# A re-ordered list of work in a fused softcap attention and maxout feed-forward kernel

## The chip, the cores and the metric

The kernel runs on one core of one Trainium2 chip. The metric is the device time of one execution in microseconds (us), the median over several runs. The kernel before takes 328.32 us (three runs, 328.07 to 328.5).

## What is computed

```python
scores = q @ k.T / sqrt(64)                # 8 batches, 12 heads, 448 x 448
scores = 30 * tanh(scores / 30)
attn   = softmax(scores)                   # over the keys
x      = (attn @ v), heads side by side    # 3584 tokens x 768
g      = maximum(x @ w1, x @ w2)           # 3584 x 1024
out    = g @ w_out                         # 3584 x 768
```

## The kernel before

**One list sets all order.** No scheduler moves anything: the string `ORDER` is a list of some 2,300 short entries, and a loop at its end calls one small function for each entry. Each function issues its instructions to fixed engines, so an engine's queue holds its instructions in the order of the list, and each engine works through its queue from the front. A dependency between two engines becomes a semaphore wait at the later instruction. The kernel is written with the identity max(a, b) = relu(a - b) + b, so that w1 - w2 feeds a relu and w2 times w_out is multiplied out beforehand.

**Units.** `t` counts 24 groups of four heads, `i` = 2t or 2t+1 counts pairs of two heads, and `g` counts 120 feed-forward groups, 14 for an even batch and 16 for an odd one.

**Entries of the attention.**
- `ld0`, `cd`: the first pairs of q and k are loaded and cast (`cd k` on VectorE, others on ScalarE). `lq`, `lk`, `lv`, `lw1`, `lw2`, `lwo` are loads by GpSimd's queue (L317, L336, L357, L364, L389).
- `X i bank` (and `Xh i c` for one half) turns q and k of a pair on TensorE (L446) for the first ten pairs, `XC` copies the result out (VectorE). From t = 5 on, `cr t` (L473) does the turning with one DMA transpose that SyncE's queue issues at L475.
- `S i j`: two score matmuls (L514) into one of only two score tiles in PSUM. `T i j` is their tanh on ScalarE (L519), `L t` and `TL t` the same for the last 64 keys (L528, L532). `E i j0 j1` and `EL t` are the exponentials on ScalarE (L536, L539). A score tile is free again when its tanh has read it.
- `A`, `B` add exponentials (VectorE), `Y` sums them on TensorE (L566, L573), `Y1` to `Y3` turn and invert the sums (VectorE), `VL`, `V` are the matmuls with v (L600, L606), and `N t u` writes the normalized result `xT` (VectorE, L618, L621).

**Entries of the weights.** `W c` turns a block of w2 on TensorE (L416), `WC` copies it out, `OP` and `P c half n` multiply it with w_out (L431), `PC` copies that out, `sub` forms w1 - w2 (VectorE). `D bank n` issues matmuls on a constant tile (L471) that only keep TensorE at work in the first 16 us.

**Entries of the feed-forward part.** `O g bank` opens group g in one of four PSUM banks. `M x y n` makes n steps, and a step is two matmuls at once (L645): one of group x on array rows 0 to 63 and one of group y on rows 64 to 127. So a group runs one half of its work on the lower rows, then the other on the upper rows, or the reverse. Both halves add into the same bank. `M x x n` uses all 128 rows (L640, the last two groups). `ev g` copies a finished group out on VectorE (L666, L702), `eva g` on ScalarE (L700). `st b t` stores rows of the output, two DMAs from SyncE's queue (L676 to L681).

**The hand-over.** When a group changes rows, its next matmul may have to wait until its last matmul on the other rows has ended. For that the entry `Hs g` puts a `nop` on SyncE's queue that waits for that last matmul, and the group's next matmul waits for the nop; `H g` puts the nop on VectorE's queue instead (L654). Where the list has no such entry ahead of a change of rows, no such wait is made (the test of `self.turn` in `step`). The list of before holds 107 `Hs` and 21 `H` for 145 changes of rows.

Of the kernel before, what the change touches and what calls it, by code (L numbers as in the profile page):

```python
# [14 lines left out]
P 1 0 4; P 3 0 2; OP 2 0 3; P 2 0 7; P 1 0 1; P 2 0 1; P 1 0 1; P 3 0 2; P 1 0 2; PC 2 0; PC 1 0; E 1 2 3;  # L15
E 1 0 2; TL 1; T 2 0; EL 0; S 3 0; S 2 2; P 3 0 1; W 0 2; P 3 0 1; X 4 3; T 2 2; T 3 0; VL 0; Y 0 1; V 0 0 0 3;
V 0 1 0 3; S 3 1; lwo 1 0; lwo 1 1; lq 5 0; lk 5 0; lv 1 0; lv 1 1; lk 8 0; lq 8 0; lq 7 0; lw2 4; lv 6 2; lq 6 0;
lk 7 0; lk 6 0; lw2 5; lw1 2; lw1 4; lw1 0; lv 2 0; lv 2 1; WC 0; PC 3 0; XC 4; Y1 0; Y2 0; Y3 0; N 0 0; N 0 1;
E 2 0 3; T 3 1; EL 1; E 3 0 2; OP 0 0 1; P 0 0 2; OP 2 1 2; P 2 1 2; P 0 0 1; OP 1 1 3; P 1 1 2; P 0 0 1; P 1 1 2;
P 0 0 1; P 1 1 4; S 4 0; S 3 2; X 5 0; P 2 1 4; P 0 0 3; P 2 1 1; XC 5; PC 1 1; PC 0 0; T 3 2; T 4 0; E 3 2 3;  # L20
OP 3 1 3; P 3 1 1; P 2 1 1; S 4 1; S 4 2; Y 1 1; T 4 1; T 4 2; L 2; P 3 1 4; VL 1; TL 2; V 1 1 0 3; V 1 0 0 3;
S 5 0; X 6 0; E 4 0 3; T 5 0; EL 2; Y1 1; Y2 1; PC 2 1; Y3 1; N 1 1; N 1 0; XC 6; X 7 2; W 4 1; S 5 2; S 5 1;
X 8 0; P 3 1 3; WC 4; XC 8; PC 3 1; T 5 1; T 5 2; OP 4 0 1; P 4 0 2; OP 0 1 0; P 0 1 3; S 6 0; S 6 1; W 5 3;
P 0 1 1; P 4 0 6; P 0 1 4; E 5 0 2; T 6 1; T 6 0; E 5 2 3; XC 7; sub 2 0; WC 5; sub 4 0; PC 4 0; sub 0 0; PC 0 1;
OP 5 1 3; P 5 1 4; S 6 2; L 3; Y 2 1; T 6 2; TL 3; E 6 0 3; VL 2; V 2 1 0 1; V 2 0 0 3; V 2 1 1 3; S 7 0; P 5 1 4;
OP 5 0 0; P 5 0 8; Y1 2; Y2 2; Y3 2; N 2 0; N 2 1; A 3 0 1; A 3 0 2; PC 5 1; PC 5 0; T 7 0; EL 3; lk 9 0; lq 11 0;
lv 3 1; lq 9 0; lw1 1; lw1 3; lq 10 0; lk 12 1; lv 3 0; lw1 5; lk 10 0; lk 11 0; lk 11 1; lk 10 1; S 7 2; O 0 1;
M 0 -1 2; S 7 1; M 0 -1 4; O 1 2; M 1 -1 1; T 7 2; T 7 1; Hs 0; M 1 -1 1; S 8 1; M 1 -1 1; M 1 0 3; S 8 0; X 9 3;
OP 4 1 0; P 4 1 4; sub 1 0; sub 3 0; XC 9; T 8 1; E 7 0 2; T 8 0; E 7 2 3; P 4 1 4; L 4; O 2 3; M 2 0 3; S 8 2;
M 2 1 3; A 3 1 1; B 3 1; PC 4 1; ev 0; B 3 0; Hs 2; TL 4; T 8 2; O 3 0; M 3 1 3; M 3 2 1; S 9 0; M 3 2 2; T 9 0;  # L30
E 8 0 3; ev 1; A 3 1 2; sub 5 0; cr 5; Hs 3; O 4 1; M 4 2 1; VL 3; V 3 0 0 3; Y 3 2; V 3 1 0 3; M 4 2 2; S 9 1;
M 4 3 3; lk 13 0; lk 13 1; lv 4 1; lv 4 0; lv 5 3; lv 5 0; lq 13 0; lq 15 0; lq 12 0; lk 12 0; lk 15 1; Y1 3;
Y2 3; Y3 3; ev 2; Hs 4; O 5 2; M 5 3 3; M 5 4 3; T 9 1; EL 4; ev 3; N 3 0; N 3 1; Hs 5; O 6 3; M 6 4 3; M 6 5 2;
S 10 0; M 6 5 1; O 7 0; M 7 5 3; Hs 6; ev 4; A 4 0 1; ev 5; M 7 6 2; S 9 2; M 7 6 1; Hs 7; cr 6; E 9 0 2; T 10 0;
T 9 2; O 8 1; M 8 6 3; S 10 2; M 8 7 3; S 10 1; O 9 2; M 9 7 1; T 10 2; T 10 1; E 9 2 3; M 9 7 2; VL 4; V 4 0 0 2;
L 5; TL 5; A 4 1 1; H 8; A 4 0 2; B 4 1; ev 7; B 4 0; A 4 1 2; ev 6; M 9 8 3; V 4 1 0 3; Y 4 0; V 4 0 2 3;
# [12 lines left out]
M 16 14 1; st 0 1; M 16 14 1; Hs 15; T 14 1; cr 8; B 6 0; M 16 15 1; S 14 2; M 16 15 1; ev 14; M 16 15 1; T 14 2;
O 17 2; M 17 15 2; H 16; M 17 15 1; B 6 1; M 17 16 2; E 13 2 3; M 17 16 1; ev 15; O 18 3; M 18 16 1; L 7; VL 6;  # L50
A 6 1 2; st 0 2; TL 7; V 6 0 0 2; V 6 1 0 2; Y 6 0; E 14 0 3; V 6 0 2 3; V 6 1 2 3; Y1 6; S 15 0; M 18 16 1;
lv 8 0; M 18 16 1; Y2 6; M 18 17 1; Y3 6; M 18 17 1; lv 8 1; M 18 17 1; O 19 0; M 19 17 2; ev 16; Hs 18; lv 8 2;
M 19 17 1; M 19 18 1; T 15 0; N 6 0; M 19 18 2; lv 8 3; O 20 1; M 20 18 2; EL 7; Hs 19; ev 17; M 20 18 1; lk 20 0;
S 15 1; M 20 19 1; N 6 1; M 20 19 1; T 15 1; M 20 19 1; lk 20 1; O 21 2; M 21 19 3; Hs 20; M 21 20 1; lq 20 0;
ev 18; M 21 20 1; S 15 2; S 16 0; ev 19; M 21 20 1; T 15 2; O 22 3; M 22 20 1; lk 21 0; M 22 20 1; A 7 0 1; Hs 21;
M 22 20 1; M 22 21 1; E 15 0 2; M 22 21 1; lk 21 1; ev 20; S 16 1; M 22 21 1; O 23 0; M 23 21 1; A 7 0 2;
M 23 21 1; Hs 22; lq 21 0; M 23 21 1; M 23 22 2; ev 21; M 23 22 1; T 16 0; M 23 22 2; A 7 1 1; M 23 22 2; cr 9;
M 23 22 1; T 16 1; M 23 22 1; B 7 0; S 16 2; M 23 22 2; B 7 1; O 24 1; M 24 22 1; T 16 2; M 24 22 2; H 23;
M 24 23 1; H 22 2; E 15 2 3; M 24 23 2; M 22 23 1; L 8; VL 7; A 7 1 2; TL 8; V 7 0 0 2; V 7 1 0 2; Y 7 2;
E 16 0 3; V 7 0 2 3; lk 22 0; V 7 1 2 3; Y1 7; S 17 0; M 22 23 1; lv 9 0; M 22 23 1; Y2 7; M 22 23 2; Y3 7;  # L60
# [145 lines left out]
def kernel(  # L206
# [21 lines left out]
    P = 128  # L228
# [550 lines left out]
```

## Time and profile before

| | |
|---|---|
| median of three runs | 328.32 us |
| span of the profiled execution, first to last instruction | 326.9 us |
| time outside the span (the difference of the two) | 1.4 us |
| ScalarE: last exponential ends | 286.9 us |
| TensorE: last matmul ends | 322.8 us |
| VectorE: last copy of results ends | 323.4 us |
| HBM traffic over the span | 180 GB/s |

The page of the profile gives each engine's busy time; the timeline lists instructions with start and length, and in brackets how long the engine was idle before and what ended that idleness. Rows marked SPq are issues by SyncE's queue: the queue is held for the length shown. A matmul's length in the rows contains the time to pass through the array, so matmuls overlap in the rows, and the distance from start to start is what each costs.

### The profile page before, as it was taken

How to read it: one execution, taken by the hardware profiler on the slowest of the kernel's cores; microseconds unless marked ns; L12 is line 12 of the kernel's file. 1: busy time of each engine (PE TensorE's matmuls, PEld its weight loads, DVE VectorE, ACT ScalarE, POOL GpSimd, SP SyncE). 2: the span in 40 equal slices, each digit the busy share in tenths (PEclk: the TensorE clock that was granted, in tenths of full speed). 3: DMA queues.
4: the chain of work that ended last, by engine and by line, in shares of the span. 5: the costliest groups of instructions: out<-in, count | busy, mean ns of one | idle time of the engine just before them, and what ended most of it. 6: DMA issues, size and time to landing. Idle time of an engine off the chain costs nothing.

```text
span 326.9 us, 9772 instructions
## 1 busy us (share of the span) xinstructions
PE 320.2 (98%) x4138; PEld 184.5 (56%) x4138; DVE 240.1 (73%) x422; ACT 281.1 (86%) x278; POOL 162.2 (50%) x237
## 2 busy tenths in 40 slices
PE   7999999999999999999999999999999999999994
PEld 3454545545656664565565565556466556557662
DVE  3346899987997778987897788968878779773201
ACT  5999999999999999999999999999999999921120
POOL 7357584568772772764774474478448311000000
PEclk9999999999999999999999999999999999999999
DMA  8999999899999999999999999999999963013033
GB/s 179 174 202 185 269 256 112 92 140 116 221 188 98 134 182 191 102 99 175 163 176 108 208 114 181 128 140 182 183 116 101 201 156 45 2 50 98 0 98 96
DMA packets 134508, 46.28 MB, mean 142 GB/s; under 512 B 112321, under 2 KB 129473, under 8 KB 134465
## 3 DMA queue, kind: packets, MB, share of 16 engines
q0 software_dynamic: 94592, 25.02, 78.3%
q1 hardware_dynamic: 39424, 19.99, 31.1%
q8 instruction: 32, 0.52, 0.6%
q10 hardware_dynamic: 448, 0.66, 0.5%
q14 instruction: 12, 0.09, 0.1%
HBM read 47.78 MB, written 11.01 MB: 180 GB/s over the span
## 4 chain that ended last, share of the span: by engine, by line
PE 93%; DMA 3%; POOL 1%; DVE 1%; issue 0%
PE mm L645 61%; PE s L514 9%; PE s L606 9%; PE mm L431 5%; DMA w2b<-in_moe_w_dram 3%; PE s L528 2%; PE s L600 2%; PE mm L573 2%; PE mm L640 1%; POOL kqs L321 1%; PE mm L458 1%; PE mm L566 1%; PE mm L416 0%; DVE xT L621 0%; POOL w2b L366 0%; DVE xT L618 0%
## 5 line engine op out<-in xcount | busy, mean ns | idle before, releaser
L519 ACT ACTIVATE e<-s 128x896 bf16<-128x896 f32 x144 | 125.5, 927 | 5.7 <-PE s L514 5.2
L536 ACT ACTIVATE e<-e 128x1792 bf16<-128x1792 bf16 (+2 forms) x72 | 122.7, 1709 | 0.0
L645 PE MATMUL mm<-wo_sb,gT 64*128 64x384 bf16 x864 | 115.2, 323 | 0.0
L645 PE MATMUL mm<-wm_sb,xT 64*128 64x384 bf16 x648 | 102.2, 323 | 0.0
L645 PE MATMUL mm<-xT,wd_sb 64*128 64x448 bf16 x768 | 97.5, 349 | 0.0
L328 POOL DMA_DIRECT2D kqs<-in_k_dram x76 | 54.7, 722 | 56.1 <-DMA qkT<-kqs 50.9
L645 PEld LDWEIGHTS <-gT 64*128 64x128 bf16 x864 | 58.6, 94 | 25.5 <-issue 1.1
L645 PEld LDWEIGHTS <-wd_sb 64*128 64x128 bf16 x768 | 48.8, 94 | 26.7 <-issue 2.1
L645 PEld LDWEIGHTS <-xT 64*128 64x128 bf16 x648 | 50.3, 94 | 18.5 <-issue 0.2
L514 PE MATMUL s<-qkT 64*128 64x448 bf16 x288 | 52.7, 352 | 0.2 <-DVE xT L618 0.2
L352 POOL DMA_DIRECT2D vp<-in_v_dram x48 | 30.5, 639 | 32.6 <-PE s L514 23.5
L666 DVE TENSOR_SCALAR gT<-mm 128x448 bf16<-128x448 f32 x64 | 38.9, 617 | 8.7 <-PE mm L645 7.6
L328 POOL DMA_DIRECT2D kqs<-in_q_dram x38 | 35.1, 924 | 5.7 <-issue 2.5
L606 PE MATMUL s<-e,vp 128*32 128x448 bf16 x576 | 36.1, 354 | 0.0
L548 DVE TENSOR_TENSOR esum<-e 128x896 bf16<-128x896 bf16 x42 | 25.9, 617 | 9.1 <-ACT e L536 9.1
L621 DVE TENSOR_TENSOR xT<-s,inv 64x448 bf16<-64x448 f32 x48 | 29.9, 622 | 1.7 <-PE s L606 0.8
L548 DVE TENSOR_TENSOR esum<-esum,e 128x896 bf16<-128x896 bf16 x42 | 26.2, 623 | 5.9 <-ACT e L536 4.8
L514 PEld LDWEIGHTS <-qkT 64*128 64x128 bf16 x288 | 18.5, 94 | 20.1 <-issue 12.0
L700 ACT COPY osb<-mm 128x384 f32<-128x384 f32 x10 | 4.8, 479 | 26.9 <-PE mm L645 26.7
L702 DVE COPY osb<-mm 128x384 f32<-128x384 f32 x44 | 23.3, 554 | 6.2 <-PE mm L645 5.7
L553 DVE TENSOR_TENSOR esum<-esum,el 64x896 bf16<-64x896 bf16 x42 | 26.0, 619 | 1.2
L578 DVE STREAM_TRANSPOSE st<-mm 128x448 f32<-128x448 f32 x24 | 15.6, 649 | 13.0 <-PE mm L573 11.3
(57 smaller groups left out, 269.7 us busy)
## 6 DMA issues: line engine op xcount, KB each, us to landing
out_dram<-osb SPq DMA_DIRECT2D x54, 192.0 KB, 4.5
vp<-in_v_dram POOLq DMA_DIRECT2D x38, 160.0 KB, 4.3
kqs<-in_q_dram POOLq DMA_DIRECT2D x46, 112.0 KB, 5.8
kqs<-in_k_dram POOLq DMA_DIRECT2D x76, 56.0 KB, 4.4
osb<-in_moe_w_dram POOLq DMA_DIRECT2D x4, 512.0 KB, 7.4
w2b<-in_moe_w_dram POOLq DMA_DIRECT2D x6, 256.0 KB, 7.1
wo_sb<-in_moe_w_out_dram POOLq DMA_DIRECT2D x4, 384.0 KB, 9.9
vp<-in_v_dram POOLq DMA_DIRECT2D x10, 128.0 KB, 7.7
```

The costliest lines, as they stand in the source:

```text
L328: nc.gpsimd.dma_start(out=to, in_=x)
L352: nc.gpsimd.dma_start(out=to, in_=x)
L514: scored[i, j] = nc.tensor.matmul(s[:, h, :S], k_of(t, o, h, j), q_of(t, o, h)).ins
L519: nc.scalar.activation(expo[i][:, 2 * j : 2 * j + 2, :], slots[i, j][:, :, :S], AF.Tanh, scale=scale / cap)
L536: nc.scalar.activation(e, e, AF.Exp, scale=float(cap))
L548: nc.vector.tensor_add(d, e[:, 0:2, :] if j == 1 else d, e[:, 2 * j : 2 * j + 2, :])
L553: nc.vector.tensor_add(d, d, left_e[t][r, :, :])
L606: nc.tensor.matmul(vals[t][place(m, u), u, :S], w[:, m, :], expo[2 * t + o][:, 2 * j + h, :], start=False, stop=(j == NJ - 1))
L621: nc.vector.tensor_mul(x[64 - r : 128 - r], vals[t][r : r + 64, u, :S], sums[t, 3][64 - r : 128 - r])
L645: ins = nc.tensor.matmul(self.ps, w[r], x[r], start=first, stop=self.at == [self.n, self.n]).ins
L666: nc.vector.tensor_relu(gT[b // 2][:, f, cs], ps)
L702: nc.vector.tensor_copy(o[:, hs], ps)
```

## The change

The string `ORDER` is written anew, and one condition in `transposes` differs. The functions are otherwise the same, and the numbers of matmuls, tanh, exponentials, loads and stores are unchanged.

**Start.** One fragment of the list per line:

```diff
-ld0 q; ld0 q 1; cd q; ld0 k; ld0 k 1; ms; dm; ms0; cd k; id; lq 2 0; lk 3 0; lq 3 0; lk 2 0; lw2 3; lw2 2; D 3 24;
-Xh 0 0 0; Xh 0 1; cd k 1 1; cd q 1 1; XCh 0 1; XCh 0 0; D 3 4; X 1 1; S 0 0; S 0 1; XC 1; T 0 0; T 0 1; D 0 5;
-D 1 8; D 3 1; D 1 4; S 0 2; D 1 4; L 0; D 1 16; T 0 2; TL 0; E 0 0 3; D 1 12; S 1 2; S 1 0; X 3 3; X 2 0; W 3 2;
-W 2 1; T 1 0; T 1 2; lw2 1; lwo 0 0; lwo 0 1; lw2 0; lq 4 0; lk 4 0; lv 0 0; lv 0 1; XC 3; XC 2; WC 3; D 0 4;
-S 1 1; D 0 8; D 2 2; S 2 1; W 1 2; WC 2; WC 1; T 1 1; T 2 1; S 2 0; D 0 4; L 1; OP 3 0 0; P 3 0 2; OP 1 0 1;
...
+ld0 q; ld0 q 1; ld0 k; ld0 k 1; ms; dm; ms0; D 3 24; id; lq 2 0; lk 3 0; lq 3 0; lk 2 0; cd k; cd q; Xh 0 0 0;
+XCh 0 0; lw2 3; Xh 0 1 1; cd k 1 1; D 3 4; lw2 2; XCh 0 1; D 2 5; cd q 1 1; S 0 0; lw2 1; D 0 4; T 0 0; S 0 1;
+lwo 0 0; X 1 2; T 0 1; lwo 0 1; S 0 2; XC 1; X 3 3; T 0 2; lw2 0; L 0; XC 3; D 2 8; TL 0; lq 4 0; D 3 16; lk 4 0;
+E 0 0 3; D 1 4; lv 0 0; D 0 4; D 3 2; D 0 8; lv 0 1; X 2 1; lwo 1 0; S 1 0; XC 2; S 1 2; T 1 0; lwo 1 1; D 0 4;
+D 3 12; lq 5 0; T 1 2; S 1 1; lk 5 0; W 3 3; T 1 1; lv 1 0; S 2 1; WC 3; W 2 2; T 2 1; lv 1 1; S 2 0; WC 2; T 2 0;
+L 1; W 1 3; TL 1; S 2 2; WC 1; E 1 2 3; S 3 0; D 3 1; OP 2 0 1; P 2 0 1; OP 3 0 2; P 3 0 1;
...
```

The first pair's two halves now go to two banks (`Xh 0 0 0`, `Xh 0 1 1`), for which `transposes` opens a bank whenever one is named:

```diff
-        if c != 1:
+        if bank is not None:
             turned["qk", i] = mm_tile(bank).bitcast(bf16)
```

**First quarter.** Up to about t = 9 and group 30 the entries stand in a new order, on TensorE, ScalarE and VectorE alike; the order of the loads among themselves is the same. The copies of groups 25, 26 and 29 move from VectorE to ScalarE (`ev` becomes `eva`).

**Rest of the list.** From `M 28 29` on, TensorE's order is the same entry for entry, but for the bank of `Y 10` (1 becomes 3), and so is ScalarE's but for the copies named below. What differs there is where the hand-overs, the transposing DMAs and the stores stand, and on which queue a hand-over is. The new list has 98 `Hs` and 47 `H`, one for each of the 145 changes of rows. Three places of one kind:

```diff
 Hs 37; cr 12; M 38 36 1; ...; O 39 0; M 39 37 1; ev 36; M 39 37 2;
-H 38; B 10 1; E 21 2 3; M 39 38 3;
+Hs 38; B 10 1; M 39 38 1; E 21 2 3; M 39 38 2;
...
 Hs 67; cr 18; M 68 66 1; ...; O 69 1; M 69 67 1; ev 66; M 69 67 2;
-H 68; B 16 1; E 33 2 3; M 69 68 3;
+Hs 68; B 16 1; M 69 68 1; E 33 2 3; M 69 68 2;
...
-Hs 81; M 82 80 1; ...; Hs 82; ...; cr 21;
+Hs 81; cr 21; M 82 80 1; ...; Hs 82;
```

**End of the list.** The copies of groups 100, 102, 103 and 112 to 117 move from ScalarE to VectorE, and most hand-overs there from SyncE to VectorE:

```diff
-Y3 23; eva 100; M 103 101 1; M 103 102 2; eva 101; M 103 102 1; N 23 0; M 103 102 3; N 23 1;
+Y3 23; M 103 101 1; M 103 102 2; eva 101; M 103 102 1; ev 100; M 103 102 3; N 23 0; st 6 1; M 103 102 3; N 23 1;
...
-M 105 103 2; eva 102; M 105 103 1; M 105 104 2; eva 103; M 105 104 1; O 106 1; M 106 104 2; Hs 105;
+M 105 103 2; ev 102; M 105 103 1; M 105 104 2; ev 103; M 105 104 1; O 106 1; M 106 104 2; st 6 2; H 105;
...
-M 115 113 2; eva 112; M 115 113 1; M 115 114 2; eva 113; M 115 114 5; st 7 3; M 115 114 4; O 116 3;
+M 115 113 2; ev 112; M 115 113 1; M 115 114 2; ev 113; M 115 114 3; st 7 3; M 115 114 6; O 116 3;
```

More of the change, by code (lines that the diff above doesn't have):

```diff
@@ L15 @@
[L15 to L24, printed above, removed]
@@ L202 @@
+M -1 117 2; Hs 116; M -1 117 1; M 116 117 8; M -1 117 2; ev 116; M -1 117 1; O 118 1; M 118 118 1; ev 117;
+M 118 118 4; st 7 5; M 118 118 9; O 119 2; M 119 119 2; ev 118; M 119 119 12; ev 119; st 7 6;
 """
```

374 lines of the change are left out of this document (197 added, 177 removed).

## Prediction

> **What bounds the kernel now.** I read the page first, for who is busy and what chain ended last.
>
> ```profile
> span 326.9 us, 9772 instructions
> PE 320.2 (98%) x4138; PEld 184.5 (56%) x4138; DVE 240.1 (73%) x422; ACT 281.1 (86%) x278; POOL 162.2 (50%) x237
> ...
> PE 93%; DMA 3%; POOL 1%; DVE 1%; issue 0%
> ```
>
> TensorE (PE) is busy 98% of the span, and 93% of the chain that ended last is its own instructions. Next the busy time by stage (columns: stretch, its length, busy us of PE, PEld, DVE, ACT, POOL, clock, DMA share, GB/s).
>
> ```profile
> 0.00:16.00 16.00, 13.63 (x185) 6.61 (x185) 4.95 (x15) 12.05 (x14) 9.42 (x20) 1.00 0.98 175
> 16.00:48.00 32.00, 31.80 (x453) 16.64 (x453) 23.29 (x40) 31.47 (x31) 20.97 (x33) 1.00 1.26 225
> 48.00:128.00 80.00, 80.00 (x1043) 45.57 (x1045) 68.25 (x119) 78.40 (x76) 48.34 (x67) 1.00 1.35 144
> 128.00:288.00 160.00, 160.00 (x2090) 93.46 (x2086) 133.39 (x234) 154.40 (x150) 83.44 (x118) 1.00 1.17 138
> 288.00:327.00 39.00, 34.78 (x377) 22.22 (x373) 10.18 (x18) 4.79 (x10) 0.00 (x0) 0.99 0.27 70
> ```
>
> ScalarE (ACT) is nearly as full up to 288 us, but then PE works on alone for 35 us. So a lead of ScalarE is no gain by itself: the end moves only where PE starts a matmul earlier or later. The numbers of matmuls are the same in both lists, so the change is worth exactly what it does to PE's waits. The view of waits shows how few those are.
>
> ```profile
> PE mm L471 <- DVE warm L734: 1.8, 1, 1.8
> PE mm L416 <- DMA w2b<-in_moe_w_dram: 0.5, 1, 0.5
> PE s L514 <- DVE xT L618: 0.2, 1, 0.2
> ```
>
> The 1.8 us at the start stays. The other two, 0.7 us, are all that this view offers a better order; shorter waits hide in the overlap of matmuls. A new wait has no such ceiling.
>
> **First quarter.** Where its waits were and how the first scores stood (PE and ACT rows of the timeline):
>
> ```profile
> 5.26 0.39 PE L471 MATMUL mm<-warm 128*128 128x512 bf16 x1
> 5.61 0.87 PE L458 MATMUL mm<-ident,kqs 64*64 64x64 bf16 x28
> 6.42 0.55 PE L514 MATMUL s<-qkT 64*128 64x448 bf16 x4
> 6.82 2.53 ACT L519 ACTIVATE e<-s 128x896 bf16<-128x896 f32 x3 [0.80 <-PE s L514]
> 10.03 2.46 ACT L536 ACTIVATE e<-e 128x2688 bf16<-128x2688 bf16 x1
> 12.36 3.37 ACT L519 ACTIVATE e<-s 128x896 bf16<-128x896 f32 x4
> 17.98 0.98 ACT L532 ACTIVATE el<-s 128x896 bf16<-128x896 f32 x1
> 15.20 0.62 PE L416 MATMUL mm<-ident,w2b 128*128 128x128 bf16 x8 [0.52 <-DMA w2b<-in_moe_w_dram]
> 16.77 3.75 PE L431 MATMUL mm<-wo_sb,w2T 128*128 128x384 bf16 x22
> 20.45 0.55 PE L514 MATMUL s<-qkT 64*128 64x448 bf16 x4
> ```
>
> The new list puts the first scores behind two warm matmuls instead of the second pair's transposes. After the first transposes (done by 5.26) come a matmul on 512 columns and one of 512 and 128: about 0.5 us, with a change of array shape, so `S 0 0` can start at about 5.84 instead of 6.42, and the first tanh, 0.40 behind it as in the rows, at 6.24 instead of 6.82. ScalarE leads by 0.58 us.
>
> What PE makes of it: tanh follow each other at (15.55 - 12.36) / 4 = 0.80 us, an exponential on 2688 columns takes 12.36 - 10.03 = 2.33. From 6.24 on, three tanh, `TL 0`, the exponential and five tanh put `TL 1` at 15.9, and it has read its score tile at 16.84. The new list lets `S 2 2` and `S 3 0` come ahead of the first `P`, and `S 3 0` needs just that tile. So PE stands from about 16.25 to 16.88, and its first `P` comes at about 17.3 instead of 16.77: 0.5 us later, with the 0.48 us of scores at 20.45 already done. The wait of 0.52 at 15.20 has gone (`W 1 3` now comes some 0.3 us after that load), one on a score tile has come. Net zero up to here.
>
> Further on the same sum by hand (PE's entries by their rows, score tiles by the tanh that frees them) keeps both lists within 0.3 us of each other until 48 us. I take -0.3 for the whole quarter: the wait of 0.2 on `xT` goes, and a little more. The bounds: -0.7, all that the view of waits offers, to +0.9, one more wait for a score tile of the length of a `TL`.
>
> Three copies go to ScalarE at about 105 to 115 us, 0.48 us each (row below): 1.44 us. ScalarE is idle for 80.00 - 78.40 = 1.6 us between 48 and 128 us and has the lead of 0.58, so they cost nothing; without that cover PE would wait up to 1.4 us at a score tile.
>
> **Hand-overs behind the transposing DMA.** Here the change adds waits, on SyncE's queue (SPq: sequencer rows; L475 is the DMA, L654 the hand-over).
>
> ```profile
> L475 SPq DMA_TRANSPOSE qkT<-kqs x19: 1296/1655/2655, 55.3 to 262.6; - x19
> DMA to landing us min/median/max: 4.2/6.7/10.0
> ...
> 55.25 1.58 SPq L475 DMA_TRANSPOSE qkT<-kqs  x1
> L654 SPq EVENT_SEMAPHORE  x1: 17/17/17, 56.9 to 56.9; - x1
> ```
>
> The issue alone holds the queue for 1.30 to 2.66 us. The last row is the stretch from 54.9 to 57.0: no hand-over comes through until the DMA's issue ends at 56.83, then one does at 56.9. Nothing on PE waited for that one. At `cr 12` and `cr 18` before, VectorE carried the hand-over while SyncE was held:
>
> ```profile
> 134.69 1.69 SPq L475 DMA_TRANSPOSE qkT<-kqs  x1
> L654 DVEq EVENT_SEMAPHORE  x1: 21/21/21, 135.6 to 135.6; - x1
> 136.03 0.75 PE L645 MATMUL mm<-wm_sb,xT 64*128 64x384 bf16 x5
> ...
> 205.01 2.27 SPq L475 DMA_TRANSPOSE qkT<-kqs  x1
> L654 DVEq EVENT_SEMAPHORE  x1: 21/21/21, 205.9 to 205.9; - x1
> 206.37 0.75 PE L645 MATMUL mm<-wm_sb,xT 64*128 64x384 bf16 x5
> ...
> L654 SPq EVENT_SEMAPHORE  x2: 17/17/17, 237.4 to 238.6; - x2
> 238.87 1.52 SPq L475 DMA_TRANSPOSE qkT<-kqs  x1
> 239.05 0.57 PE L645 MATMUL mm<-wm_sb,xT 64*128 64x384 bf16 x4
> 160.28 1.27 SPq L681 DMA_DIRECT2D out_dram<-osb  x2
> ```
>
> The PE rows are the first matmuls that need the hand-over (groups 38, 68, 82). With `Hs 38` and `Hs 68` the nop stands behind the DMA: free at 134.69 + 1.69 = 136.38 and 205.01 + 2.27 = 207.28, plus about 0.1 to pass the nop and reach PE, so PE stands 0.45 and 1.0 us. `cr 21` now follows the hand-over at 237.4; with the same 0.27 us from hand-over to issue as at 238.6 it begins at 237.7, and the matmul at 239.05 has 1.35 us for issue and passage, as in the other two. PE's queue stops there: the matmul of the other group behind it, the scores and the sums all wait. The mean of the issues in the rows over the 1.25 us that fit is about 0.5 (19 issues: 0.05 at 1.30, 1.4 at 2.66). Three make 1.5; PE then comes later to two sums and score tiles for which it waits a little now, which I put at -0.3. Taken: +1.2. Bounds: +0.1 if all three issues are near 1.3, +3.5 if all are near 2.6. By the steps that lie between in the list, the other hand-overs behind a `cr` have over 2 us, and those behind a store about the 1.27 us that its two DMAs take; nearly all of the 17 added ones come many steps after the group's last matmul on the other rows, so their nop has long gone through. Those moved to VectorE cost it 21 ns each where it is idle 15% (68.25 of 80): zero.
>
> The Trainium skill, page "DMA: Bandwidth & Descriptors", section "Issuing engines are not separate DMA queues", speaks against this: the sequencer's time to initiate a DMA is usually small relative to the DMA. Here the row has 1.66 us of 6.7. By the page, with that time at nil, the +1.2 would be 0 and the sum 328.2; I go by the row.
>
> **End.** `ev 100` moves ahead of the last normalizations on VectorE:
>
> ```profile
> L702 DVE COPY osb<-mm 128x384 f32<-128x384 f32 x44 | 23.3, 554 | 6.2 <-PE mm L645 5.7
> L700 ACT COPY osb<-mm 128x384 f32<-128x384 f32 x10 | 4.8, 479 | 26.9 <-PE mm L645 26.7
> ...
> 291.80 1.26 DVE L621 TENSOR_TENSOR xT<-s,inv 64x448 bf16<-64x448 f32 x2
> 293.41 0.35 PE L645 MATMUL mm<-xT,wd_sb 64*128 64x448 bf16 x1
> 320.59 0.56 DVE L705 COPY osb<-mm 128x384 f32<-128x384 f32 x1 [15.46 <-PE mm L640]
> ```
>
> The normalization then ends at 293.06 + 0.55 = 293.61, and the group's sixth step at 293.41 needs it: +0.2. The other eight copies run 0.075 us longer on a VectorE that is idle for 15.46 us before the last two copies: zero, since the banks they free are taken over 1 us later.
>
> **Sum.** -0.3 + 1.2 + 0.2 = +1.1 on a span of 326.9: 328.0. Outside the span lie 328.32 - 326.9 = 1.4 us, taken as unchanged, so I set the sum against the median: 329.4.
>
> **Rivals.**
> - *The quarter pays and the hand-overs just fit.* The three issues take 1.3 us, as the quickest of the 19, and cost 0.2 together; ScalarE's lead of 0.58 takes with it the small waits on tanh that hide in overlapping matmuls, 1.0 us more beside the 0.7. For it: the lead is sure. Against: PE waited for tanh nowhere for long. 328.3 - 1.7 + 0.2 + 0.2 = 327.0.
> - *Nothing reaches the end.* The change doesn't do what it says: new waits for score tiles eat the quarter's gain, and PE, stopped at a hand-over, would have stopped at the next sum anyway. 328.4.
> - *ScalarE falls behind.* The three copies meet a ScalarE without its lead; from about 105 us each score waits until its 1.6 us of idleness have made it up. This decides if the lead at 90 us is under 0. 328.3 + 1.4 + 1.2 + 0.2 = 331.1.
>
> **How the numbers follow.** Forecast 329.4 with 0.44 (its own range 328.99 to 330.5), the quarter pays 0.22, nothing 0.22, ScalarE behind 0.12. The bound of what this measurement can tell is 0.2%, 0.66 us: 327.66 and 328.98. Faster is the first rival, 0.22; within the bound is the second and a sliver of the forecast, 0.24; slower the rest, 0.54. Signs are mixed, so the range has to reach both: from 327.1, near the first rival, to 331.2, the third.
>
> **What would show it.** In the new profile: the first tanh at about 6.2; no wait on w2b at 15.2 but PE standing before the scores near 16.5; and the three places, where the matmul of groups 38, 68 and 82 starts right behind the end of a DMA_TRANSPOSE issue. If PE runs through there while the issue is still held, the middle term is wrong; if the hand-overs stop PE and the time is still lower, the first quarter was undervalued.

## The result and the profile after

The new list takes 333.36 us (median of four runs, 333.1 to 336.2), the old one 328.28 beside it: a ratio of 1.0167, with a 95% interval of 1.0145 to 1.0188. It is slower by about 5 us, where 1.1 were forecast. (The medians alone give 1.0155; the ratio takes in the execution of 336.2 as well.) One execution of a later kernel, `e4_three_vec`, counts as slow (336.61 us) and is left out of its ratio, though not of its median. The profiled execution of after is the quickest of the four (333.1 us). First its page:

```profile
span 331.3 us, 9789 instructions
PE 321.8 (97%) x4138; PEld 188.4 (57%) x4138; DVE 243.7 (74%) x428; ACT 278.4 (84%) x272; POOL 161.7 (49%) x237
...
PE 83%; DVE 9%; ACT 3%; DMA 3%; issue 1%; SPq 0%; DVEq 0%
```

The same 4138 matmuls are spread over 4.4 us more. TensorE's own share of the chain that ended last falls from 93% to 83%, and VectorE (DVE) and ScalarE (ACT) now stand in it: TensorE has begun to wait for others. The busy time by stage says where (columns as before):

```profile
16.00:48.00 32.00, 30.86 (x453) 16.50 (x447) 22.23 (x38) 30.41 (x29) 20.91 (x33) 1.00 1.25 224
48.00:128.00 80.00, 78.69 (x992) 44.87 (x990) 65.53 (x113) 78.08 (x79) 48.08 (x67) 1.00 1.39 137
128.00:288.00 160.00, 159.13 (x2083) 91.10 (x2084) 132.49 (x233) 153.97 (x149) 83.21 (x118) 1.00 1.17 141
```

TensorE stood still for 1.14, 1.31 and 0.87 us in stages where it had stood still for 0.20, 0 and 0. From 48 to 128 us it started 992 matmuls in place of 1043. The clock (1.00) is the same in these stages. The view of waits names the stops:

```profile
PE s L523 <- DMA qkT<-kqs: 1.0, 1, 1.0
PE mm L654 <- SPq L663: 0.9, 2, 0.6
PE mm L467 <- issue: 0.5, 1, 0.5
PE s L523 <- ACT el L541: 0.4, 1, 0.4
PE s L523 <- DVE xT L627: 0.3, 1, 0.3
PE s L537 <- ACT e L528: 0.3, 1, 0.3
PE mm L582 <- DVE gT L675: 0.2, 1, 0.2
```

Lines here are those of before plus 9 (L523 is the score, L654 the feed-forward matmul, L663 the hand-over, L484 the transposing DMA). The wait on w2b is gone as forecast, and the one on `xT` has moved. The second row is the forecast's SyncE term. The first and third were in no term.

How far TensorE is behind the execution of before can be followed through the whole run. For each execution I summed the time by which matmuls start later than the ones ahead of them allow, and compared two executions where they have done the same amount of matmul work. The us lost against before, by the time in before (the rows of two later experiments stand here for comparison; the trace of `e6_five_cr7` lacks the record of one of the first warm matmuls, which is counted in):

| time in before, us | 25 | 40 | 75 | 85 | 120 | 125 | 140 | 220 | 240 | 300 |
|---|---|---|---|---|---|---|---|---|---|---|
| after | 0.3 | 0.8 | 1.0 | 2.4 | 3.0 | 3.4 | 3.5 | 3.5 | 4.4 | 4.4 |
| `e6_five_cr7` | -0.1 | 0.2 | 0.4 | 0.6 | 1.1 | 1.3 | 1.3 | 1.3 | 1.3 | 1.3 |
| `e12_all_moves` | 0.6 | 1.1 | 1.1 | 1.2 | 1.6 | 1.6 | 1.6 | 1.8 | 1.8 | 1.9 |

So 3.4 us of the 4.4 are lost by 125 us, in the first quarter, which was forecast to gain 0.3. The rest of the list loses 1.0, and the end nothing.

**The start.** Timeline of after, TensorE:

```profile
5.34 0.98 PE L480 MATMUL mm<-warm 128*128 128x512 bf16 x3
6.25 0.36 PE L523 MATMUL s<-qkT 64*128 64x448 bf16 x2
...
17.27 0.37 PE L523 MATMUL s<-qkT 64*128 64x448 bf16 x2 [0.39 <-ACT el L541]
17.57 0.23 PE L480 MATMUL mm<-warm 128*128 128x128 bf16 x1
17.64 0.65 PE L440 MATMUL mm<-wo_sb,w2T 128*128 128x384 bf16 x3
```

The three warm matmuls ahead of the first score take 6.25 - 5.34 = 0.91 us, not 0.5, so the score gains 0.17 us on before, not 0.58. Another execution with the same list up to here, that of `e6_five_cr7` (below), has it otherwise:

```profile
5.26 0.66 PE L472 MATMUL mm<-warm 128*128 128x512 bf16 x3
5.88 0.37 PE L515 MATMUL s<-qkT 64*128 64x448 bf16 x2
```

There the three take 0.62 us, and the score comes at 5.88, where 5.84 was forecast. What differs is TensorE's granted clock. In every trace the warm matmuls on 512 columns start 0.43 us apart at first and 0.22 us apart later, and the trace's clock record sets in, at full speed, at the turn: at 5.00 us in before, at 6.02 in after, at 4.44 here. It lies between 5.0 and 6.2 us in the four executions that begin with the old list and between 4.4 and 7.8 in the ten that begin with the new one; the traces don't tell whether the list has a part in it.

The stop at `S 3 0` behind `TL 1` is there as forecast, at 17.27, and the first `P` comes at 17.64 (forecast 17.3). In the two executions whose clock was full before 5 us (`e4_three_vec`, `e6_five_cr7`) it comes at 17.31 and 17.27. So the 0.3 us that after has lost by 25 us belong to this execution's clock.

**The largest stop.** SyncE's queue and the score of pair 14 in after, then the landing of that one transposing DMA (`cr 7`):

```profile
75.51 1.18 SPq L690 DMA_DIRECT2D out_dram<-osb  x2
76.98 1.77 SPq L484 DMA_TRANSPOSE qkT<-kqs  x1
...
86.68 0.37 PE L523 MATMUL s<-qkT 64*128 64x448 bf16 x2 [0.97 <-DMA qkT<-kqs]
```

```profile
DMA to landing us min/median/max: 9.6/9.6/9.6
```

Before, the two issues stood in the other order:

```profile
75.82 2.20 SPq L475 DMA_TRANSPOSE qkT<-kqs  x1
78.07 2.19 SPq L681 DMA_DIRECT2D out_dram<-osb  x2
```

There the tile landed 7.8 us after its issue, at 83.6, and the score at 84.32 did not wait. In the new list the store `st 0 0` is ahead. It waits for its copy until 75.5 us, and `cr 7` behind it goes out at 76.98, 1.2 us later than before. TensorE is itself about as late there: without the stop the score would come 0.16 us behind the matmul at 85.38, about 85.5, so from issue to score there are 8.5 us in both lists. The tile is late because it takes 9.65 us to land instead of 7.82. Had the DMA gone out ahead of the store, it would have had more room; `e3_cr7_first` below tries that.

**The hand-overs.** The three places of the forecast in after, SyncE and TensorE:

```profile
138.03 1.72 SPq L484 DMA_TRANSPOSE qkT<-kqs  x1
139.86 0.66 PE L654 MATMUL mm<-wm_sb,xT 64*128 64x384 bf16 x5 [0.23 <-SPq L663]
...
208.52 1.30 SPq L484 DMA_TRANSPOSE qkT<-kqs  x1
209.93 0.69 PE L654 MATMUL mm<-wm_sb,xT 64*128 64x384 bf16 x5
...
241.21 2.12 SPq L484 DMA_TRANSPOSE qkT<-kqs  x1
243.44 0.66 PE L654 MATMUL mm<-wm_sb,xT 64*128 64x384 bf16 x5 [0.64 <-SPq L663]
```

In each, the first matmul that needs the hand-over starts 0.11 us behind the end of the issue (138.03 + 1.72 = 139.75, then 139.86). An issue of 1.30 us just fits, one of 2.12 does not. From start to start the stops cost 0.45, 0 and 0.85 us (the brackets count only the time in which the array had run empty).

### The profile page after: what moved, and what is told of

Its sections match the earlier page's. It is cut to its first block, busy times and chain, and to the rows that moved or that the text cites. A ratio compares the mean times of both kernels' runs of the same rounds, so it can differ in the third digit from the quotient of the medians.

```text
span 331.3 us, 9789 instructions
## 1 busy us (share of the span) xinstructions
PE 321.8 (97%) x4138; PEld 188.4 (57%) x4138; DVE 243.7 (74%) x428; ACT 278.4 (84%) x272; POOL 161.7 (49%) x237
## 4 chain that ended last, share of the span: by engine, by line
PE 83%; DVE 9%; ACT 3%; DMA 3%; issue 1%; SPq 0%; DVEq 0%
PE mm L654 56%; PE s L523 8%; PE s L615 8%; DMA qkT<-kqs 3%; PE mm L440 3%; DVE wd_sb L411 2%; ACT e L528 2%; PE s L537 2%; PE mm L582 1%; PE mm L649 1%; PE s L609 1%; PE mm L480 1%; DVE xT L630 1%; DVE wm_sb L446 1%; PE mm L467 1%
## 5 line engine op out<-in xcount | busy, mean ns | idle before, releaser
L654 PE MATMUL mm<-wo_sb,gT 64*128 64x384 bf16 x864 | 116.2, 323 | 0.0
L654 PE MATMUL mm<-wm_sb,xT 64*128 64x384 bf16 x648 | 103.4, 323 | 0.9 <-SPq L663 0.9
L654 PE MATMUL mm<-xT,wd_sb 64*128 64x448 bf16 x768 | 98.3, 349 | 0.0
L654 PEld LDWEIGHTS <-gT 64*128 64x128 bf16 x864 | 60.6, 94 | 22.9 <-issue 1.1
L654 PEld LDWEIGHTS <-wd_sb 64*128 64x128 bf16 x768 | 49.2, 94 | 27.1 <-issue 1.5
L654 PEld LDWEIGHTS <-xT 64*128 64x128 bf16 x648 | 50.4, 94 | 19.6 <-SPq L663 2.2
L523 PE MATMUL s<-qkT 64*128 64x448 bf16 x288 | 54.4, 353 | 1.8 <-DMA qkT<-kqs 1.0
L711 DVE COPY osb<-mm 128x384 f32<-128x384 f32 x50 | 27.0, 554 | 18.6 <-PE mm L654 18.1
L615 PE MATMUL s<-e,vp 128*32 128x448 bf16 x576 | 35.3, 354 | 0.0
L523 PEld LDWEIGHTS <-qkT 64*128 64x128 bf16 x288 | 18.8, 94 | 21.2 <-issue 11.7
L541 ACT ACTIVATE el<-s 128x896 bf16<-128x896 f32 x24 | 22.1, 922 | 2.8 <-PE s L537 2.3
```

The costliest lines, as they stand in the source:

```text
L523: scored[i, j] = nc.tensor.matmul(s[:, h, :S], k_of(t, o, h, j), q_of(t, o, h)).ins
L615: nc.tensor.matmul(vals[t][place(m, u), u, :S], w[:, m, :], expo[2 * t + o][:, 2 * j + h, :], start=False, stop=(j == NJ - 1))
L654: ins = nc.tensor.matmul(self.ps, w[r], x[r], start=first, stop=self.at == [self.n, self.n]).ins
L711: nc.vector.tensor_copy(o[:, hs], ps)
```

## The experiments

Ratios are to the kernel before on the same chip. For scale: 1.001 is 0.33 us. "Quad t" is the group of four heads t, whose transposing DMA is `cr t`. Lines in the rows move by a few from kernel to kernel.

### Which part of the list carries the loss

Both lists do the same work up to the sum of quad 9, so they can be cut there and joined.

```diff
 E 20 0 3; M 32 31 1;
-Y 9 2; ...; M 39 37 2; Hs 38; B 10 1; M 39 38 1; E 21 2 3; M 39 38 2; ...
+Y 9 2; ...; M 39 37 2; H 38; B 10 1; E 21 2 3; M 39 38 3; ...
```

> The new list up to the sum of group 9 (about 129 us in the profile of after), the old list from there on, so the old hand-overs at groups 38, 68 and 82 and the old end. Theory (the first quarter lost about 3.3 us by the time both lists meet, the rest about 1.0): 328.3 + 3.3 = 331.6, between 331.2 and 332.1. Rival, the prediction's own split (first quarter -0.3, the rest everything): 328.0, at most 329.2. Rival that the loss of the quarter is made up again once the old hand-overs follow: under 330.5.

Measured: 332.21 us, ratio 1.0106 (1.0079 to 1.0133).

The reverse, old up to there and new behind it:

```diff
 E 20 0 3; M 32 31 1;
-Y 9 2; ...; M 39 37 2; H 38; B 10 1; E 21 2 3; M 39 38 3; ...
+Y 9 2; ...; M 39 37 2; Hs 38; B 10 1; M 39 38 1; E 21 2 3; M 39 38 2; ...
```

> The old list up to the sum of group 9, the new one from there on. Theory: the waits behind the transposing DMA at groups 38 and 82 (0.45 and 0.85 us in the profile of after, 0.25 of it made up at the next sum), nothing at group 68 and nothing at the end: 328.3 + 1.0 = 329.3, between 328.9 and 329.7. Rival, the prediction's own terms for the rest (+1.2 and +0.2): 329.7. Rival that the rest carries nearly all of the loss: over 331.5. All three places may come out otherwise than in after, as the landing of loads shifts by 3 us against the rest: then the wait at group 68 may come instead.

Measured: 330.29 us, ratio 1.0058 (1.0039 to 1.0077). The excesses, 1.06% and 0.58%, add up to 1.64%, where the whole change has 1.67%. Within these intervals the two parts add: the quarter costs 3.5 us, the rest 1.9. The rest's row of waits:

```profile
PE mm L642 <- SPq L651: 1.5, 2, 0.8
```

It loses nothing else that this view shows. The quarter's 3.5 us are near the theory's 3.3, though its median lies just above the stated range (332.1). The rest is larger than the theory's 1.0 and above its range (329.7): here the hand-overs of groups 38 and 82 stop TensorE's array for 0.66 and 0.83 us, in after for 0.23 and 0.64.

### The order of a store and a transposing DMA

```diff
-st 0 0; M 11 10 1; S 12 1; ...; M 12 11 1; cr 7; T 12 1;
+cr 7; st 0 0; M 11 10 1; S 12 1; ...; M 12 11 1; T 12 1;
```

> After, with one entry moved: the transposing DMA of quad 7 is issued ahead of the first store instead of behind it. In after, the store waits for its copy until 75.5 us and the DMA goes out at 76.99 and lands at 86.63, 1.16 us late for the score of pair 14. Theory (the order on SyncE's queue is what makes it late): the issue comes at 74 to 75.5, the landing by 85, the wait of 1.16 on PE is gone, and the time falls by 0.9 to 1.2 us to 332.2 to 332.5. Rival (the DMA waits for loads or for the queues of the DMA engines, not for the store): landing stays at 86 to 87, the time at 333.4. Rival that the store moved behind now makes its buffer late: a wait of VectorE on the output tile, time 333.4 or more.

Measured: 332.27 us, ratio 1.0111 (1.009 to 1.0133), 1.8 us better than after, where both ratios are known to about 0.7 us. SyncE's queue and the score in its profile:

```profile
73.80 1.74 SPq L476 DMA_TRANSPOSE qkT<-kqs  x1
75.70 1.18 SPq L682 DMA_DIRECT2D out_dram<-osb  x2
...
85.70 0.38 PE L515 MATMUL s<-qkT 64*128 64x448 bf16 x2
```

```profile
DMA to landing us min/median/max: 6.0/6.0/6.0
```

Issued 3.2 us sooner, the tile lands 6.0 us later instead of 9.6, at 79.8, and the score has no wait. So the order on the queue decides whether TensorE waits here; what makes the landing itself longer or shorter is not shown (last section). That the profiled span is 331.3 here too comes from other causes in that execution: the clock is full only at 7.82 us, and the first `P` comes 0.8 us later than in after (18.40), and hand-overs cost 0.83, 0.78 and 0.93.

### The hand-overs on SyncE

```diff
-Hs 38; ... Hs 68; ... Hs 82;
+H 38; ... H 68; ... H 82;
```

> After, with the hand-overs of groups 38, 68 and 82 that stand behind a transposing DMA on SyncE given back to VectorE. Theory: the waits of PE on SyncE's queue at 139.9 (0.45, of which 0.25 was made up) and 243.4 (0.85) go, -1.0 us: 332.4, between 332.1 and 332.7; at group 68 nothing changes as nothing waited. Rival, that PE would have stopped at the next sum or score anyway: 333.1 to 333.4. Rival that the hand-over on VectorE comes late behind its own work (B entries of 0.6 us stand there): 333.4 or more.

Measured: 331.64 us, ratio 1.0087 (1.0061 to 1.0114), 2.6 us better than after, where the theory had 1.0. Its profile shows two more stops of the kind that I had not seen:

```profile
122.90 3.19 SPq L476 DMA_TRANSPOSE qkT<-kqs  x1
126.19 0.74 PE L646 MATMUL mm<-xT,wd_sb 64*128 64x448 bf16 x6 [0.39 <-SPq L655]
...
215.81 2.77 SPq L476 DMA_TRANSPOSE qkT<-kqs  x1
218.67 1.18 SPq L682 DMA_DIRECT2D out_dram<-osb  x2
219.96 0.33 PE L646 MATMUL mm<-wm_sb,xT 64*128 64x384 bf16 x1 [0.40 <-SPq L655]
```

The first stands behind `cr 11`, the second (group 71) behind `cr 19` and the store `st 4 0` together. The next kernel moves the five that I took for the places so far:

```diff
-Hs 20; ... Hs 31; ... Hs 38; ... Hs 71; ... Hs 82;
+H 20; ... H 31; ... H 38; ... H 71; ... H 82;
```

> After, with the five hand-overs that stood behind a transposing DMA or a store in the traces so far and stopped PE (groups 20, 31, 38, 71, 82) on VectorE. Theory: waits behind SyncE's queue are the whole loss of the rest and a part of the quarter's; in the four runs with new hand-overs they came to 0.2 to 1.0 us each. The ratio to before falls from 1.0167 (after) by some 2.5 us to 1.009 or below, and no wait on SyncE's hand-over line over 0.15 us is left; left over are the late transposed tile at 86 us (0.8 to 1.2), waits on VectorE and the stall in the transposes at 37 us. Rival: the stalls only move to the next sum or score, ratio 1.014 or more. Against the run with three moved (1.0087): 0.3 to 0.9 us less.

Measured: 331.7 us, ratio 1.0119 (1.0082 to 1.0156), runs from 329.76 to 334.53. No better than with three, where 0.3 to 0.9 us less and a ratio of 1.009 at most were expected. Against after it is 1.6 us, for five hand-overs that hold the three, so what the three cost in a usual execution is not settled closer than by these two runs. The stops behind SyncE are gone but for one of 0.2 us at 149 us. In this execution the late tile of quad 7 cost its full price, and that wait alone may make the scatter:

```profile
85.98 0.36 PE L515 MATMUL s<-qkT 64*128 64x448 bf16 x2 [0.98 <-DMA qkT<-kqs]
```

One of the five was named wrongly: the matmul at 126 us belongs to group 30, not 31. Both changes together:

```diff
-Hs 20; ... Hs 31; ... Hs 38; ... Hs 71; ... Hs 82;
+H 20; ... H 31; ... H 38; ... H 71; ... H 82;
-st 0 0; M 11 10 1; ...; M 12 11 1; cr 7;
+cr 7; st 0 0; M 11 10 1; ...; M 12 11 1;
```

> After, with the five hand-overs of groups 20, 31, 38, 71 and 82 on VectorE and quad 7's transposing DMA ahead of the first store as well. Theory: the two causes are separate places and add up, 0.8 to 1.2 us less than with the five hand-overs alone: ratio 1.004 to 1.006 (329.7 to 330.3 us at 328.4 for before). What is left is then VectorE's waits (about 1.4 us more than before in the quarter) and, in some executions, 0.65 us of stall at 37 us. Rival: ScalarE sets the pace once these waits go, so that new waits on tanh come in: ratio stays at 1.008 or more, with rows of scores waiting for ScalarE over 0.5 us.

Measured: 330.55 us, ratio 1.0072 (1.0057 to 1.0087), runs within 2 us again. Against the five hand-overs alone, quad 7's order is worth 0.47%, 1.5 us, with both ratios known to 0.15 and 0.37%. That agrees with the 1.8 us above, so the two causes add up as far as this can tell; what is left is a little more than expected. No wait on ScalarE appears that after does not have, so the rival falls.

### The first scores ahead, alone

```diff
-XCh 0 1; XCh 0 0; D 3 4; X 1 1; S 0 0; S 0 1; XC 1; T 0 0;
+XCh 0 1; XCh 0 0; D 3 4; S 0 0; S 0 1; X 1 1; XC 1; T 0 0;
```

> Before, with one thing of the change alone: the first two scores ahead of the second pair's transposes. The copy that the score needs ends at 6.07 us in the profile of before, so the score comes at about 6.1 in place of 6.42 and ScalarE starts 0.35 us sooner. Theory (PE is the bound, and ScalarE's lead is worth nothing by itself): 328.0 to 328.5, no difference that can be told. Rival, the prediction's best case (the lead pays): up to 0.35 us less, and the small waits on tanh with it, under 327.8. Rival (the second pair comes late): score of pair 1 later than 10.6 us and the time above 328.8.

Measured: 328.91 us, ratio 1.0023 (1.0012 to 1.0034): slower, by 0.75 us. Rows of TensorE, ScalarE and VectorE:

```profile
6.38 0.55 PE L509 MATMUL s<-qkT 64*128 64x448 bf16 x4 [0.47 <-DVE qkT L458]
...
7.53 0.62 DVE L458 COPY qkT<-mm 128x896 bf16<-128x896 bf16 x1 [1.21 <-PE mm L453]
...
8.21 0.86 PE L466 MATMUL mm<-warm 128*128 128x512 bf16 x3 [0.34 <-DVE qkT L458]
...
9.41 0.92 ACT L514 ACTIVATE e<-s 128x896 bf16<-128x896 f32 x1 [0.90 <-PE s L509]
```

The score comes at 6.38, hardly sooner than before (6.42): the copy that it needs ends at 6.32, where before's profile has 6.05, since the first transposes began 0.2 us later here. The second pair's transposes are now later, so is their copy out of the PSUM bank (7.53), and the warm matmuls that use that bank wait for it at 8.21. Score tile 2 stands behind them, and ScalarE idles 0.90 us. The theory and the best case were both wrong here, and the last rival, that the second pair comes late, showed both its signs: the first score of pair 1 comes at 11.55 us, and the time is above 328.8. In the new list, with another order of the warm matmuls, ScalarE has no such pause.

### The three copies on ScalarE

```diff
-eva 25; ... eva 26; ... eva 29;
+ev 25; ... ev 26; ... ev 29;
```

> After, with the three copies that went to ScalarE (groups 25, 26, 29) back on VectorE at their places in the new list. Theory (they lie in ScalarE's slack): the time of after, ratio 1.015 to 1.019. Rival, the prediction's third case (ScalarE without a lead, 1.4 us): ratio 1.012 or less, and the waits of the scores at about 115 and 128 us on ScalarE's copies (0.17 and 0.19 us with the change of shape in after) gone. Second rival, that VectorE, which is busier there, becomes late with normalizations: 1.019 or more.

Measured: 333.35 us, ratio 1.016 (1.0147 to 1.0174). The time of after: the copies cost nothing where they are. Its profile is of the slowest of its runs (336.76) and shows how far the late tile of quad 7 can go. Below the score's row stand two stretches of the busy time behind it (columns as above, the clock third from the end):

```profile
87.88 0.36 PE L515 MATMUL s<-qkT 64*128 64x448 bf16 x2 [2.36 <-DMA qkT<-kqs]
...
89.00:92.50 3.50, 3.50 (x24) 2.70 (x20) 1.90 (x4) 2.33 (x3) 3.50 (x6) 0.51 1.40 89
92.50:96.00 3.50, 3.50 (x61) 2.07 (x57) 2.35 (x5) 3.30 (x5) 0.54 (x1) 1.00 1.99 180
```

The late tile costs about 2.5 us. Then the granted clock is at half from 89.06 to 92.48 us (0.51 in the first stretch), which costs about another 1.5. No other trace has such a fall between the start and the end, and none has a wait as long (1.0 us at most behind the start), so the wait probably brought it about; one execution doesn't show it.

### What else the quarter waits for

On top of `e6_five_cr7`, five places where TensorE waited for VectorE:

```diff
-S 3 2; lk 7 0; S 4 0; T 3 2; P 2 1 2;
+lk 7 0; S 4 0; P 2 1 2; S 3 2; T 3 2;
-Y 3 2; V 3 1 0 3; V 3 0 0 3;
+V 3 1 0 2; Y 3 2; V 3 1 2 3; V 3 0 0 3;
-S 9 2; T 10 0; M 7 6 1; lk 15 1; M 7 6 1; ev 5;
+T 10 0; M 7 6 1; lk 15 1; M 7 6 1; S 9 2; ev 5;
-S 11 2; M 8 9 2; ... S 13 2; H 12; ev 11; M 14 13 2;
+M 8 9 1; S 11 2; M 8 9 1; ... H 12; ev 11; M 14 13 2; S 13 2;
```

> After with the five hand-overs on VectorE and quad 7's transposing DMA first, and five small moves against PE's waits on VectorE in the first quarter: four scores (pair 3 tile 2, pair 9 tile 2, pair 11 tile 2, pair 13 tile 2) one or two steps later, the sum of quad 3 behind half of a value step. In the profile with the first two changes the waits at 27.1, 57.4, 63.2, 72 and 83.9 us are 0.46, 0.37, 0.30, 0.2 and 0.24 us, of which about 0.1 each is the change of shape. Theory (those waits are the rest of the quarter's loss, and PE is the bound): 0.8 to 1.1 us less than without the moves, ratio 1.0035 to 1.005. Rival (the moved scores make ScalarE late, or the waits only go to the next score): ratio 1.007 as without them. Third: below before's time, ratio under 0.999, if the list was better but for its waits.

Measured: 330.36 us, ratio 1.006 (1.0047 to 1.0073). Less than half of what was expected. Of the waits that were covered, some came back at the next instruction that needs VectorE: one matmul later, at 63.82 us, the next feed-forward matmul waits 0.39 us for a relu on VectorE, which stands behind the normalization in VectorE's queue. So here an engine that is late was not outrun by moving one reader.

Three more moves on top, with the right group 30:

```diff
-Hs 30; ... L 1; W 1 3; TL 1; ... S 3 0; D 3 1; OP 2 0 1; P 2 0 1; OP 3 0 2; P 3 0 1;
+H 30; ... W 1 3; L 1; TL 1; ... D 3 1; OP 2 0 1; P 2 0 1; OP 3 0 2; P 3 0 1; S 3 0;
```

> The run with the scores later (after, five hand-overs on VectorE, quad 7's transposing DMA first, five moves in the first quarter), and three more: the hand-over of group 30, the one that really stands behind quad 11's transposing DMA (0.33 us of wait at 124.6 there, and 0.87 in the run with more matmuls), on VectorE; the transposes of w2's chunk 1 ahead of the left-over score at 15.4 us (0.46 of wait on ScalarE); the first score of pair 3 behind two premultiplication steps (0.56 of wait at 17.0). Theory (the new list loses by named waits alone): 0.33 + 0.36 + 0.3 = about 1.0 us less than with the scores later (1.006), ratio 1.0025 to 1.004. Rival (a part of the loss is no wait at all: short pauses at changes of shape, and ScalarE): ratio 1.005 or more. Third: under 1.001, as good as before, if the named waits were all.

Measured: 329.85 us, ratio 1.0036 (1.0023 to 1.0048), as the theory said. All moves together take away 1.3% of the 1.67%, 4.3 of 5.5 us, without touching the matmuls' number or kind. What is left, 1.2 us in the median, stays open. Of the 1.9 us in the profiled execution (table above) 0.6 are lost in the first 25 us, and 0.4 is the stop that the last experiment is about. Its clock was full only at 7.21 us, 2.2 us later than in before, and half of that, 1.1 us, is the most that this can cost, so the 0.6 need not be the list's.

The other way round, two of before's own waits covered:

```diff
-W 4 1; S 5 2; S 5 1; X 8 0; P 3 1 3;
+W 4 1; P 3 1 1; S 5 2; S 5 1; X 8 0; P 3 1 2;
-V 4 1 0 3; Y 4 0; V 4 0 2 3;
+V 4 1 0 3; V 4 0 2 3; Y 4 0;
```

> Before, with two of its own waits on VectorE covered: the score at 36.6 us (0.33 us on a normalization) one step of the premultiplication later, and the sum of quad 4 at 68 us (0.22) behind the value step that follows it. Theory: 0.2 to 0.35 us less than before, ratio 0.999 to 0.9995, which is at the edge of what can be told. Rival: the waits go elsewhere, ratio 1.000 or more.

Measured: 328.61 us, ratio 1.0005 (0.9992 to 1.0019). Nothing that can be told. No version that I ran beats before.

### A stop without a semaphore

In after, TensorE stops inside a row of 56 equal transposes, and nothing is waited for:

```profile
35.80 0.91 PE L467 MATMUL mm<-ident,kqs 64*64 64x64 bf16 x45
37.17 0.35 PE L467 MATMUL mm<-ident,kqs 64*64 64x64 bf16 x11 [0.46 <-issue]
```

The kernel for this is after with 45 more, smaller warm matmuls at the start:

```diff
-D 2 8; ... D 3 16; ... D 3 12;
+D 2 1; D 2 1; D 2 1; D 2 1; D 2 1; D 2 1; D 2 1; D 2 1; ... D 3 1; D 3 1; D 3 1; D 3 1; ...
```

> After, with 15 warm matmuls on 512 columns at the start cut into 60 on 128 columns: 45 more matmuls, 90 more instructions of PE, and no other change. It asks what stops PE for 0.65 us in the middle of the transposes of pair 7 at 37.2 us, where no semaphore is waited for. Theory: the next 16 KB block of PE's own instructions, which is fetched by DMA. In the profile of after, a packet of 16 KB lands at 35.7 us, 1.45 us before PE goes on, and PE goes on at its matmul 45 of the 56 transposes of pairs 6 and 7. With 90 more instructions the same block begins 45 matmuls earlier, so if PE stops it is at the start of the transposes of pair 6, and not inside pair 7. Rival (the transposes themselves, their bank or their data): the stop stays at the same transpose of pair 7. It is seen in two of four traces of the new list so far, so that it may be absent here, which would leave it open. Time: that of after, give or take 1 us.

Measured: 332.42 us in a single execution. The transposes run through:

```profile
36.34 1.07 PE L462 MATMUL mm<-ident,kqs 64*64 64x64 bf16 x56
```

No stop at the old place, nor at the new one, so the place was not tested; what the packets say of it stands in the last section.

## Why the prediction was right or wrong

**What bounds the kernel: right.** "The change is worth exactly what it does to PE's waits" held: the number of matmuls is the same, and so is the clock but for its start, the gain of waits removed showed in the time (`e3_cr7_first`, `e4_three_vec`, `e12_all_moves`), and ScalarE's share of the work moved without effect (`e8_ev_vec`). So did "a new wait has no such ceiling".

**ScalarE's lead at the start: right for a clock that is full by 5 us.** Forecast 0.58 us, measured 0.16 in after (first tanh at 6.66). The sum took 0.2 us for a warm matmul on 512 columns, as in before's rows from 5.26 us on; in after the first two took 0.40 and 0.36, because the clock was full only at 6.02. With the clock full by about 5.0, as in before, the lead is 0.42 to 0.53 (first tanh at 6.29 to 6.40 in `e4_three_vec`, `e6_five_cr7` and `e9_scores_later`). That the clock's start differs from execution to execution was in no term. The lead's worth for the end was rightly put at little; in the old list the earlier scores alone cost 0.75 us (`e7_old_scores_first`).

**The first 25 us: right.** The w2b wait has gone, the stop behind `TL 1` has come, and the 0.3 us lost where 0 were forecast are the clock's. (The terms given for `TL 1` add up to 15.8 us, not 15.9, which changes nothing.)

**The first quarter: the step that failed.** "Further on the same sum by hand keeps both lists within 0.3 us of each other until 48 us. I take -0.3 for the whole quarter": the sum ended at 48 us, where after had already lost 0.8 us, and for TensorE's waits in the 75 us behind it there was no working (but for the three copies), only the bound of "one more wait for a score tile". The part cost 3.5 us by `e1_first_new`, far past that bound of +0.9. Shown by the runs, in the order of size: the transposing DMA of quad 7 behind a store that waits (1.2 us in the profile, 1.5 to 1.8 by the ratios), waits on VectorE and ScalarE that the new order uncovers together with group 30's hand-over (1.2 us between `e6_five_cr7` and `e12_all_moves`, for eight moves at once, so not shared out among them), and in some executions the stop in the transposes (0.4 to 0.65). About 1.2 us of the whole change is left with all these moves, and its cause stays open. The first stands on SyncE's queue, and I had looked at that queue only for hand-overs, not for what its DMAs are late for.

**The hand-overs in the rest: right in kind, in size within its bounds.** Forecast +1.2 with bounds of +0.1 and +3.5 (by its own rows the upper one is 3 x (2.6 - 1.25) - 0.3 = 3.75). The profile shows 0.45 + 0 + 0.85, less 0.2 made up at the sum of quad 10; `e2_rest_new` puts the usual cost at 1.9. So it is partly luck that the profile's 1.1 comes so near to 1.2: the issue at group 68 happened to take 1.30 us. The sentence that "the other hand-overs behind a `cr` have over 2 us" was wrong for two: group 30 behind `cr 11`, whose issue held the queue for 2.8 us in after, and group 71, where the DMA and a store add up. The Trainium skill's rule (page "DMA: Bandwidth & Descriptors", section "Issuing engines are not separate DMA queues"), by which the time to initiate a DMA is usually small beside the DMA itself, does not hold for this DMA: its issue takes 1.66 of 6.7 us to landing in before and 1.71 of 6.2 in after (medians), and taking hand-overs out of its way gained 2.6 us with three and 1.6 us with five (`e4_three_vec`, `e5_five_vec`).

**The three copies on ScalarE, the end: right and harmless.** Zero for the copies, as forecast. The +0.2 at the last normalization did not come: the loss is 4.32 us at the last sum and 4.4 at the end.

**Outside the span:** 333.1 - 331.3 = 1.8 us, where 1.4 were taken. It is 1.8 in the executions of before as well (328.27 us with a span of 326.5): the 1.4 set the median against the span of another execution, which by this took about 328.7 us. With the quick execution that after's profile shows, that is why the profiles differ by 4.4 us and the medians by 5.1.

**The rivals.** "ScalarE falls behind" came nearest in time (331.1) for a reason that is refuted (`e8_ev_vec`). No rival held a late DMA in the first quarter.

## What to carry to other kernels

When an order is rewritten, follow every queue that the rewrite touches to what its entries are late for, to the end of the rewritten part; a sum that stops half-way is no estimate of the other half. On a queue that issues DMAs, an entry that waits (a store for its copy) delays all behind it, and a DMA that issues slowly holds up even a `nop`: put the DMA whose landing is needed ahead of the store, and semaphore hand-overs on a queue that issues nothing slow. In a kernel at 98% of its bounding engine a reordering can lose more than it can gain: here the view of waits offered 0.7 us, and the new order lost 5. And before two profiles of a kernel's start are compared, look at when the clock is full in each.

## What the runs showed of the hardware

**A transposing DMA's issue** took 1.30 to 2.66 us in before. In the 14 traces together, 16 of 266 issues begin 0.3 us behind the last DMA of a store: they took 1.69 to 3.42 us, with a median of 2.68, the others 1.30 to 2.95, with a median of 1.70. It is plainest at `cr 11`: 1.29 to 1.36 us in the four executions of the old first quarter, 2.50 to 3.42 in the ten of the new one, where the list has a store right ahead of it.

**The time to landing** of quad 7's DMA went with the time of its issue: 5.3 to 6.0 us when issued at 73.2 to 73.9 us (four executions, ahead of the store), 7.0 to 8.2 at 75.1 to 76.0 (four, old first quarter) and 7.8 to 11.0 at 76.0 to 77.2 (six, behind the store). So in the new list a later issue was paid for twice. Whether the store's own transfers or the loads at that time hold it up is not shown; at `cr 11` a store right ahead doesn't lengthen the landing (6.2 to 8.0 us with it, 6.6 to 7.5 without).

**The granted clock** at the start doubles TensorE's speed at a time that differs from execution to execution, 4.4 to 7.8 us here (warm matmuls 0.43 us apart until then, 0.22 afterwards).

**The stop without a semaphore** looks like TensorE's own instructions. The page of after counts their DMA:

```profile
q8 instruction: 32, 0.52, 0.6%
```

The trace has these packets one by one: 16,384 bytes each, one for every 252 instructions of TensorE on the average. The Trainium skill (page "Runtime: NRT & Kernel Launch", section "Instruction fetch mechanics") says that the sequencer fetches instructions in blocks of 16 KiB, 256 of them, by a DMA queue of its own, and that this is mostly hidden. The size agrees; the stop may be a place where it is not hidden. It sits at the same transpose, 45 done and 11 to go, in four executions of lists with the new first quarter, and each time TensorE goes on 1.4 to 1.5 us after such a packet has landed. Here it is in the last kernel:

```profile
36.35 0.91 PE L459 MATMUL mm<-ident,kqs 64*64 64x64 bf16 x45
37.44 0.35 PE L459 MATMUL mm<-ident,kqs 64*64 64x64 bf16 x11 [0.18 <-issue]
```

| execution | packet landed, us | TensorE at that transpose, us | later by | stop, us |
|---|---|---|---|---|
| after | 35.72 | 37.17 | 1.45 | 0.65 |
| `e1_first_new` | 35.93 | 37.41 | 1.48 | 0.64 |
| `e6_five_cr7` | 35.15 | 36.60 | 1.45 | 0.43 |
| `e12_all_moves` | 36.06 | 37.44 | 1.38 | 0.37 |
| `e3_cr7_first` | 35.84 | 37.36 | 1.52 | none |
| `e5_five_vec` | 34.86 | 36.46 | 1.60 | none |
| `e4_three_vec` | 34.36 | 36.20 | 1.84 | none |
| `e8_ev_vec` | 34.34 | 36.98 | 2.64 | none |
| `e9_scores_later` | 33.92 | 36.57 | 2.65 | none |

Where the packet came at least 1.5 us ahead, there was no stop. The packet starts 2 to 4 us after TensorE has entered the block before, among the loads that fill the DMA engines there (224 GB/s from 16 to 48 us), and the transposes use up instructions fast: 56 of them, with as many weight loads, in 1.07 us (row of the experiment above). That the fetch causes the stop is argued from these records; the one kernel that moved the block's edge had its packet 8.5 us ahead and shows no such stop, so it doesn't settle it.
